# A Mamba-2 scan and a hard-swish MLP on one core: the first MLP product from three products of 12-bit parts instead of seven half-products

## The chip, the core and the metric

The kernel runs on one core of one Trainium2 chip. The core has five engines that run side by side and meet through semaphores: in this kernel PE multiplies matrices into PSUM (used as eight banks of 128 partitions by 512 float32 values), ACT and DVE work element by element on SBUF and PSUM, POOL works element by element on SBUF, and SP only issues DMAs. PEld is the row of PE's weight loads: a matmul has a loaded operand, here of up to 128x128, and an operand that is streamed past it, here of up to 512 columns. The metric is the device time of one execution in microseconds.

## What is computed

Two stages follow each other. The first is a Mamba-2 scan of 4 batches, 8 heads, 768 positions, head width 32 and state width 16. The second is an MLP over the 3072 resulting rows of 256 values:

```python
h = x @ w_in                     # 3072x256 times 256x2048
relu6 = np.clip(h + 3.0, 0.0, 6.0)
g = h * relu6 / 6.0
return (g @ w_out)               # 3072x2048 times 2048x256
```

The weights come in as float64 and are decoded on the chip to float32; x, a, B and C are float32. The change is about `x @ w_in`.

## The kernel before

The 768 positions are cut into 6 blocks of 128; with 4 batches a block holds 512 rows of the MLP. Block k has three kinds of work, and the program interleaves them by hand: the scan of the block after it (k+1) and preparations for the one after that (k+2) are put between the products of the MLP of block k. The order of the instructions on each engine is the order in which the program writes them; nothing is planned by a scheduler.

**Block 0** is simple. `mlp_in` (line 621) makes h in 16 slices of 128 columns (f = 0 to 15), each from two float32 matmuls (two, as 256 input values are two halves of 128, j = 0 and 1), while the weights are still being decoded by `decode` (line 189). `first_out` (line 711) then makes the output product, four batches times four weight chunks, one step (i, b) after the other; between the steps the loop in the last part of the program puts the scan of block 1, four calls for sums of w_out (`weight_sums`, line 737) and two calls for sums of w_in (`in_weight_sums`, line 640).

**Blocks 1 to 5** make the first product by a seven-product scheme (a Strassen form on 2x2 blocks). Two slices of h belong to one step s (0 to 7), one even and one odd. Each of the four parts (even or odd, first or second 256 of the 512 rows) is a sum over j; instead of eight half-products of 256 columns, `lead`, `early`, `middle` and `last` (lines 669 to 698) issue seven through `half_product`, some on sums of weights (tile w_sum and two temporary ones) and sums of rows (tile ts, by `sum_y`, line 656), and ACT and DVE carry intermediate sums between the banks. `lead` of the next step runs one step ahead, and `lead(c, 0)` of the next block is put near the end of the previous block's output product. A step holds two PSUM banks; three pairs of banks rotate (f0/f2, f1/f3, y0/y1).

The slice h then goes through `ramp` (line 700, ACT: relu of h/6 + 1/2 into the tile gT) and `times_ramp` (line 705, DVE: the minimum with 1, times h). POOL makes sums of these slices for the output product (`g_sums`, line 756), which is a seven-product scheme too: `wide_units` (line 835) for blocks 1 to 4 and `out_units` (line 768) for block 5. While `wide_units` yields its steps i = 0 to 13, the loop puts in the scan of the next block: `scores` and `multiply` at i = 2 or 3, `decay_ends` of the block after it (32 short exponentials on ACT and 4 products on POOL in all) at i = 2 to 5, `results` (`mix` on PE, `keep` with four copies by ACT into yT, and `sum_y`) at i = 6 or 7, and `turn_all` at i = 9.

The loads go through SP's queue in program order: `load_bc` (B once with tokens first, and 16 DMAs that bring C and B in squares), `load_x`, and `rows` (the decay rows L and eto). The stores of a block, 32 of them, go through the same queue. The pools `loads` and `att` have two buffers for each tag unless a tile says otherwise.

Of the kernel before, what the change touches and what calls it, by code (L numbers as in the profile page):

```python
# [11 lines left out]
BF16 = mybir.dt.bfloat16  # L12
AF = mybir.ActivationFunctionType
# [7 lines left out]
def kernel(  # L21
# [24 lines left out]
    nc = tc.nc  # L46
# [38 lines left out]
    def load_bc(c):  # L85
# [21 lines left out]
        Bs[c] = tokens_first(B, nc.scalar if c == 0 else nc.sync, name="B")  # L107
        if c == 0:
            bcs[c] = [pairs_first(C), Bs[c]]
        elif c < TURN:  # L110
            bcs[c].append(Bs[c])
        elif c > TURN:
            bcs[c] = [pairs_first(C), pairs_first(B)]
        else:
            return lambda: bcs.update({c: [pairs_first(C), pairs_first(B)]})

    def load_x(c):
        sl = slice(c * P, (c + 1) * P)
        xts[c] = loads.tile([P, NB * NH, D], FP32, name="xt")
        nc.sync.dma_start(out=xts[c], in_=x[:, :, sl, :].rearrange("b h s d -> s (b h) d"))  # L120

    w_in = const.tile([P, NK, DF], FP32, name="w_in")
    w_sum = const.tile([P, NF // 2, P], FP32, name="w_sum")
    w_out = const.tile([P, NF, DM], FP32, name="w_out")
    NP = 4
    FP = NF // NP
    NRAW = 3
# [61 lines left out]
    def decode(i):  # L189
# [42 lines left out]
        if i < NP:  # L232
            dst = w_in[:, :, i * FP * P:(i + 1) * FP * P]
# [159 lines left out]
    def ends(c, b):  # L393

        if b == 0:
            bss[c] = att.tile([P, G, N], FP32, name="bs")
# [214 lines left out]
    def keep(c):  # L611

        yTs[c] = att.tile([P, NK, NB, P], FP32, name="yT")
# [7 lines left out]
    def mlp_in(k, f):  # L621
        h = ps.tile([P, NK, 2 * P], FP32, name="h", tag=f"f{f % 4}")
        for j in range(NK):
            nc.tensor.matmul(  # L624
                out=h.rearrange("p r i -> p (r i)"), lhsT=w_in[:, j, f * P:(f + 1) * P],
# [11 lines left out]
    wi = w_in.rearrange("p k (j e c) -> p k e j c", e=2, c=P)  # L637
    in_sums, y_sums, evens, odds, parts_of = {}, {}, {}, {}, {}

    def in_weight_sums():  # L640
        for h in range(2):
            js = slice(h * NJ // 2, (h + 1) * NJ // 2)
            a11, a12, a21, a22 = (wi[:, k, e, js] for e in range(2) for k in range(2))
            s1, s2 = (att.tile([P, NJ // 2, P], FP32, name="w_sum", tag=t) for t in ("ws", "we"))
            s4 = w_sum[:, js]
            for o, p_, q_, op in ((s1, a21, a22, ALU.add), (s2, s1, a11, ALU.subtract),
                                  (s4, a12, s2, ALU.subtract), (a21, a11, a21, ALU.subtract)):
                nc.vector.tensor_tensor(out=o, in0=p_, in1=q_, op=op)
            for n, t in ((1, s1), (2, s2), (3, a21), (4, s4)):
# [487 lines left out]
```

## Time and profile before

| what | value |
|---|---|
| median of 3 runs | 354.44 us (354.25 to 355.27) |
| the profiled execution | 354.35 us, of which the span of its instructions is 352.6 us |
| PE busy | 344.0 us, 98% of the span |
| DVE, ACT, POOL busy | 228.7, 179.4, 138.8 us (65%, 51%, 39%) |
| first product of blocks 1 to 5 (PE chain, tiles even and odd) | 20.1% and 14.7% of the span |
| granted PE clock | 0.999 of full speed |

In a row of the groups, the numbers are the tile written and the tiles read, the shapes, the count, the busy time in us, the mean duration of one in ns, and after the bar the idle time of the engine just before. A matmul's duration includes its passage through the array, so it is longer than the distance between the starts of two matmuls in a row; the distance is what a stream of them costs, and it is read from the chain, where a stretch of PE work has a length and a count. For ACT and DVE the same is read from the starts in the timeline.

### The profile page before, as it was taken

The page shows a single profiled execution, that of the slowest core. Times are in us where ns is not written, and L with a number is a line of the kernel's source. Part 1 is how long each engine was busy: PE and PEld are TensorE (multiplying, and loading weights), DVE is VectorE, ACT ScalarE, POOL GpSimd, SP SyncE. Part 2 cuts the span into 40 slices and gives each one's busy share as a digit, 9 for nine tenths or more (in the row PEclk, how much of TensorE's full clock was granted, in tenths as well). Part 3 has the DMA queues.
Part 4 walks back from the last instruction along what each step waited for, and adds up shares of the span by engine and source line. Part 5 has one row for each costly group of instructions (what it writes and reads, how often), then busy time and mean ns, then how long its engine had stood idle before and what let it go on. Part 6 is the DMA issues. An engine that isn't in the chain of part 4 may idle for free.

```text
span 352.6 us, 8499 instructions
## 1 busy us (share of the span) xinstructions
PE 344.0 (98%) x3448; PEld 281.9 (80%) x3448; DVE 228.7 (65%) x426; ACT 179.4 (51%) x394; POOL 138.8 (39%) x139
## 2 busy tenths in 40 slices
PE   6899999999999999999999999999999999999996
PEld 2554458888888888888888888888888888888996
DVE  6699999975788628786438787436787322688111
ACT  3778887258775731664741565551575011466100
POOL 3300000362499612099513099610078600068700
PEclk9999999999999999999999999999999999999999
DMA  8988979602900293255034256001200001200000
GB/s 168 190 301 166 214 268 149 86 16 77 164 1 6 57 167 70 35 69 83 2 82 91 35 67 90 4 4 17 34 9 0 2 5 19 37 7 0 2 30 32
DMA packets 89607, 25.18 MB, mean 71 GB/s; under 512 B 82208, under 2 KB 85952, under 8 KB 89056
## 3 DMA queue, kind: packets, MB, share of 16 engines
q1 hardware_dynamic: 85184, 23.33, 35.3%
q10 hardware_dynamic: 4384, 1.31, 1.7%
q8 instruction: 27, 0.44, 0.6%
q14 instruction: 12, 0.10, 0.1%
HBM read 21.33 MB, written 3.29 MB: 70 GB/s over the span
## 4 chain that ended last, share of the span: by engine, by line
PE 94%; DMA 3%; DVE 1%; SPq 1%; issue 0%; DVEq 0%
PE even L666 20%; PE odd L666 15%; PE wb L844 12%; PE wc L844 8%; PE o L721 8%; PE h L624 8%; PE wa L844 8%; PE oa L780 4%; PE ob L780 4%; PE y L602 3%; PE y L505 2%; PE cb L532 2%; DMA raw<-in_moe_w_in_dram 2%; DMA pairs<-in_C_dram 1%; PE y L546 1%; SPq L100 1%
## 5 line engine op out<-in xcount | busy, mean ns | idle before, releaser
L766 POOL TENSOR_TENSOR s<-gT 128x512 f32<-128x512 f32 x20 | 25.4, 1271 | 82.4 <-DVE gT L707 82.4
L666 PE MATMUL even<-ts,w_sum 128*128 128x256 f32 x160 | 48.1, 382 | 0.0
L702 ACT ACTIVATE gT<-odd,half 128x512 f32<-128x512 f32 x40 | 27.5, 688 | 33.8 <-DVE odd L695 33.8
L666 PE MATMUL odd<-yT,w_in 128*128 128x256 f32 x160 | 41.1, 379 | 0.0
L681 ACT COPY even<-odd 128x512 f32<-128x512 f32 x40 | 23.0, 574 | 27.7 <-PE odd L666 25.0
L666 PEld LDWEIGHTS even<-ts,w_sum 128*128 128x128 f32 x160 | 30.0, 190 | 5.1 <-ACT up L688 1.3
L707 DVE SCALAR_TENSOR_TENSOR gT<-gT,odd 128x512 f32<-128x512 f32 x40 | 27.5, 688 | 9.9 <-ACT gT L702 9.9
L666 PEld LDWEIGHTS odd<-yT,w_in 128*128 128x128 f32 x160 | 30.4, 190 | 4.1
L387 ACT ACTIVATE L<-L,cum_n 128x64 f32<-128x64 f32 x128 | 31.5, 340 | 0.0
L844 PE MATMUL wb<-s,w_out 128*128 128x256 f32 x128 | 30.7, 382 | 0.0
L707 DVE SCALAR_TENSOR_TENSOR gT<-gT,even 128x512 f32<-128x512 f32 x40 | 27.2, 679 | 4.4 <-ACT gT L702 4.4
L702 ACT ACTIVATE gT<-even,half 128x512 f32<-128x512 f32 x40 | 27.8, 695 | 4.4 <-PE even L666 4.4
L721 PE MATMUL o<-w_out,gT 128*128 128x256 f32 x128 | 28.7, 381 | 0.0
L405 POOL TENSOR_TENSOR tmp<-state,eto 128x256 f32<-128x256 f32 x5 | 3.4, 684 | 62.1 <-ACT eto L391 62.1
L624 PE MATMUL h<-yT,w_in 128*128 128x512 f32 x64 | 27.7, 594 | 0.0
L721 PEld LDWEIGHTS o<-w_out,gT 128*128 128x128 f32 x128 | 24.1, 190 | 3.7 <-issue 0.5
L682 DVE COPY up<-odd 128x256 f32<-128x256 f32 x40 | 16.9, 424 | 15.4 <-ACT even L681 14.6
L844 PEld LDWEIGHTS wb<-s,w_out 128*128 128x128 f32 x128 | 24.0, 190 | 3.4
L766 POOL TENSOR_TENSOR s<-s,gT 128x512 f32<-128x512 f32 x20 | 25.9, 1295 | 1.6
L766 POOL TENSOR_TENSOR gT<-gT 128x512 f32<-128x512 f32 x20 | 25.5, 1274 | 0.0
L766 POOL TENSOR_TENSOR s<-gT,s 128x512 f32<-128x512 f32 x20 | 25.5, 1273 | 0.0
L160 POOL TENSOR_SCALAR_AFFINE_SELECT L<-L 64x1024 f32<-64x1024 f32 (+1 forms) x16 | 18.9, 1182 | 15.3 <-DMA L<-cum_d 14.9
(150 smaller groups left out, 666.1 us busy)
## 6 DMA issues: line engine op xcount, KB each, us to landing
raw<-in_moe_w_out_dram SPq DMA_DIRECT2D x4, 1024.0 KB
L<-cum_d SPq DMA_DIRECT2D x8, 512.0 KB
xt<-in_x_dram SPq DMA_DIRECT2D x6, 512.0 KB
raw<-in_moe_w_in_dram SPq DMA_DIRECT2D x3, 1024.0 KB
out_dram<-back SPq DMA_DIRECT2D x128, 16.0 KB
pairs<-in_C_dram SPq DMA_DIRECT2D x40, 32.0 KB
eto<-cum_e SPq DMA_DIRECT2D x20, 64.0 KB
B<-in_B_dram SPq DMA_DIRECT2D x5, 256.0 KB
```

The source lines that it names most:

```text
L160: nc.gpsimd.affine_select(out=t[rows], in_=t[rows], pattern=pattern, compare_op=ALU.is_ge, fill=-1e5, base=base, channel_multiplier=-1)
L387: nc.scalar.activation(Ls[c][:, b, h], Ls[c][:, b, h], AF.Exp, bias=cum_n[:, c, g:g + 1])
L624: nc.tensor.matmul(out=h.rearrange("p r i -> p (r i)"), lhsT=w_in[:, j, f * P:(f + 1) * P], rhs=yTs[k][:, j].rearrange("p b i -> p (b i)") ...
L666: nc.tensor.matmul(out=bank[:, r], lhsT=lhsT, rhs=rhs, start=start, stop=True, skip_group_check=True)
L681: nc.scalar.copy(out=even, in_=odd[:, 1:2].to_broadcast([P, 2, 2 * P]))
L682: nc.vector.tensor_copy(out=up[:, 1], in_=odd[:, 0])
L702: nc.scalar.activation(gTs[k][:, f], h.rearrange("p r i -> p (r i)"), AF.Relu, bias=half, scale=1.0 / 6.0)
L707: nc.vector.scalar_tensor_tensor(out=g, in0=g, scalar=1.0, in1=h.rearrange("p r i -> p (r i)"), op0=ALU.min, op1=ALU.mult)
L721: nc.tensor.matmul(out=o[:, b % 2], lhsT=gTs[0][:, f, b * P:(b + 1) * P], rhs=w_out[:, f], start=(f == 0 and b % 2 == 0), stop=True, skip_ ...
L766: nc.gpsimd.tensor_tensor(out=o, in0=p_, in1=q_, op=op)
L780: nc.tensor.matmul(out=bank[:, slot], lhsT=lhs[:, j], rhs=rhs[:, j], start=(clear and j == 0), stop=True, skip_group_check=True)
L844: nc.tensor.matmul(out=bank[:, slot], lhsT=lhs[:, j], rhs=rhs[:, j], start=(clear and j == 0), stop=True, skip_group_check=True)
```

## The change

In blocks 1 to 5 the seven-product scheme of the first product goes. Each operand x is split in two parts of 12 bits, hi = x(1 - e/2) rounded to the type float32r with e = 2^-12, and lo = x - hi; the lo of the weights is multiplied by 1/e. A third operand, called less, combines the two: lo - hi of the weights (with the scaled lo), and e hi - lo of the rows. For each slice f there are three products with 512 streamed columns and two halves j each: hi times hi and lo times lo into one bank (`squares`), then that bank is multiplied in place by 1 + e on ACT, or on DVE for every fourth slice and the first two of block 1 (`enlarge`), and then less times less is accumulated on it (`cross`). That sum is hi hi + hi lo + lo hi + lo lo. All these matmuls have float32r operands; in the kernel before no matmul has.

Slices run in the order squares(f), cross(f-2), enlarge(f), factor(f-2), with six banks in rotation; `factor` is `ramp` and `times_ramp`. `lead` now means the first two slices' squares. The split of the weights (`in_parts`, four chunks in two parts each) is put between the steps of block 0's output product, and the split of the rows (`split_y`) takes the place of `sum_y`. The tiles B, xt, bs and yT have one buffer instead of two, w_in becomes four tiles that the parts of later chunks overwrite, ob, res, x1 and u of the outputs share tags with tiles of `wide_units`, and t2 and t4 of the w_out sums get buffers of their own. Loads move: x of the next block is loaded at slice 2 of a block, where before x of the block after it was; B and C of block 2 are loaded after step (1, 3) of block 0. The four w_out sums move from block 0 (and one from block 1's output product) to slices 4, 7, 9 and 12 of block 1. In block 0, conceal, turn, wake, decay and ends are put at other steps, and in later blocks `decay_ends` is one step later (i = 3 to 6).

```diff
-        Bs[c] = tokens_first(B, nc.scalar if c == 0 else nc.sync, name="B")
+        Bs[c] = tokens_first(B, nc.scalar if c == 0 else nc.sync, name="B", bufs=1)
         if c == 0:
             bcs[c] = [pairs_first(C), Bs[c]]
         elif c < TURN:
             bcs[c].append(Bs[c])
-        elif c > TURN:
+        else:
             bcs[c] = [pairs_first(C), pairs_first(B)]
-        else:
-            return lambda: bcs.update({c: [pairs_first(C), pairs_first(B)]})
 
     def load_x(c):
         sl = slice(c * P, (c + 1) * P)
-        xts[c] = loads.tile([P, NB * NH, D], FP32, name="xt")
+        xts[c] = loads.tile([P, NB * NH, D], FP32, name="xt", bufs=1)
...
-    w_in = const.tile([P, NK, DF], FP32, name="w_in")
-    w_sum = const.tile([P, NF // 2, P], FP32, name="w_sum")
-    w_out = const.tile([P, NF, DM], FP32, name="w_out")
     NP = 4
     FP = NF // NP
+    w_in = [const.tile([P, NK, FP * P], FP32, name="w_in", tag=f"w{i}") for i in range(NP)]
...
-            bss[c] = att.tile([P, G, N], FP32, name="bs")
+            bss[c] = att.tile([P, G, N], FP32, name="bs", bufs=1)
...
-        yTs[c] = att.tile([P, NK, NB, P], FP32, name="yT")
+        yTs[c] = att.tile([P, NK, NB, P], FP32, name="yT", bufs=1)
...
-    def sum_y(k):
-        ts = att.tile([P, 3, 2 * P], FP32, name="ts", bufs=1)
-        t1, t2, t4 = (ts[:, i] for i in range(3))
-        t3 = y_half(k, 0, 1)
-        y_sums[k] = {1: t1, 2: t2, 3: t3, 4: t4}
-        for o, p_, q_ in ((t1, t3, y_half(k, 0, 0)), (t3, y_half(k, 1, 1), t3),
-                          (t2, y_half(k, 1, 1), t1), (t4, y_half(k, 1, 0), t2)):
-            nc.vector.tensor_tensor(out=o, in0=p_, in1=q_, op=ALU.subtract)
...
-    def half_product(bank, r, lhsT, rhs, start=False):
-        nc.tensor.matmul(
-            out=bank[:, r], lhsT=lhsT, rhs=rhs, start=start, stop=True, skip_group_check=True)
-
-    def lead(k, s):
...
-        half_product(odd, 1, wi[:, 0, 0, s], y_half(k, 0, 0), start=True)
-        half_product(odd, 0, in_sums[3][s], y_sums[k][3])
-        nc.scalar.copy(out=even, in_=odd[:, 1:2].to_broadcast([P, 2, 2 * P]))
-        nc.vector.tensor_copy(out=up[:, 1], in_=odd[:, 0])
-
-    def early(k, s):
-        even = evens[k, s]
-        half_product(even, 0, wi[:, 1, 0, s], y_half(k, 1, 0))
-        half_product(even, 1, in_sums[2][s], y_sums[k][2])
-        nc.scalar.copy(out=parts_of[k, s][:, 0], in_=even[:, 1])
-
-    def middle(k, s):
-        even, odd, up = evens[k, s], odds[k, s], parts_of[k, s]
-        half_product(odd, 0, wi[:, 1, 1, s], y_sums[k][4])
-        half_product(even, 1, in_sums[1][s], y_sums[k][1])
-        nc.vector.tensor_tensor(out=odd[:, 0], in0=odd[:, 0], in1=up[:, 0], op=ALU.add)
-        nc.vector.tensor_tensor(out=odd[:, 1], in0=even[:, 1], in1=up[:, 1], op=ALU.add)
-
-    def last(k, s):
-        half_product(evens[k, s], 1, in_sums[4][s], y_half(k, 1, 1))
+    EPS = 2.0 ** -12
+    w_parts, y_parts, hs_ = {}, {}, {}
+
+    def in_parts(i):
+        n = FP * P
+
+        def one(pool, tag):
+            t = pool.tile([P, NK, n], F32R, name="w_part", tag=tag)
+            return [t[:, j] for j in range(NK)]
+
+        def two(tag):
+            return [att.tile([P, n], F32R, name="w_part", tag=tag) for _ in range(NK)]
+
+        hi = one(const, f"w{i - 1}" if i else "hi")
+        lo = one(const, f"lo{i}") if i < 2 else one(att, "wm") if i == 2 else two("ws")
+        less = one(const, f"less{i}") if i < 2 else one(att, "wm") if i == 2 else two("we")
+        for j in range(NK):
+            nc.scalar.activation(hi[j], w_in[i][:, j], AF.Copy, scale=1.0 - EPS / 2)
+            (nc.vector if j and i > 1 else nc.gpsimd).tensor_tensor(
+                out=lo[j], in0=w_in[i][:, j], in1=hi[j].bitcast(FP32), op=ALU.subtract)
+        yield
+        for j in range(NK):
+            nc.scalar.activation(lo[j], lo[j].bitcast(FP32), AF.Copy, scale=1.0 / EPS)
+            nc.vector.tensor_tensor(
+                out=less[j], in0=lo[j].bitcast(FP32), in1=hi[j].bitcast(FP32), op=ALU.subtract)
+        w_parts[i] = (hi, lo, less)
+        yield
+
+    def split_y(k):
+        hi = const.tile([P, NK, TB], F32R, name="y_hi", tag=f"w{NP - 1}")
+        lo = att.tile([P, NK, TB], F32R, name="y_lo", bufs=1)
+        less = att.tile([P, NK, TB], F32R, name="y_less", bufs=1)
+        for j in range(NK):
+            y = yTs[k][:, j].rearrange("p b i -> p (b i)")
+            nc.scalar.activation(hi[:, j], y, AF.Copy, scale=1.0 - EPS / 2)
+            nc.vector.tensor_tensor(
+                out=lo[:, j], in0=y, in1=hi[:, j].bitcast(FP32), op=ALU.subtract)
+            nc.vector.scalar_tensor_tensor(
+                out=less[:, j], in0=hi[:, j].bitcast(FP32), scalar=EPS,
+                in1=lo[:, j].bitcast(FP32), op0=ALU.mult, op1=ALU.subtract)
+        y_parts[k] = (hi, lo, less)
+
+    def part_products(k, f, n, m, start=False):
+        w, y = w_parts[f // FP][n], y_parts[k][m]
+        for j in range(NK):
+            nc.tensor.matmul(
+                out=hs_[k, f], lhsT=w[j][:, f % FP * P:(f % FP + 1) * P], rhs=y[:, j],
+                start=(start and j == 0), stop=True, skip_group_check=True)
+
+    def squares(k, f):
+
+        pool, tag = ((ps, "f0"), (ps, "f1"), (ps, "f2"), (ps, "f3"), (ps_y, "y0"), (ps_y, "y1"))[f % 6]
+        hs_[k, f] = pool.tile([P, TB], FP32, name="h", tag=tag)
+        part_products(k, f, 0, 0, start=True)
+        part_products(k, f, 1, 1)
+
+    def enlarge(k, f):
+
+        h = hs_[k, f]
+        if f % 4 == 3 or k == 1 and f < 2:
+            nc.vector.tensor_scalar(
+                out=h, in0=h, scalar1=1.0 + EPS, scalar2=None, op0=ALU.mult)
+        else:
+            nc.scalar.activation(h, h, AF.Copy, scale=1.0 + EPS)
+
+    def cross(k, f):
+        part_products(k, f, 2, 2)
+
+    def factor(k, f):
+        ramp(k, f, hs_[k, f])
+        times_ramp(k, f, hs_[k, f])
+
+    def lead(k):
+        for f in range(2):
+            squares(k, f)
+            enlarge(k, f)
...
-                lead(c, 0)
+                lead(c)
...
-            ob = ffn.tile([P, 2, DM], FP32, name="ob", bufs=2)
+            ob = ffn.tile([P, 4, DM], FP32, name="ob", tag=("wide", "back")[b // 2])[:, :2]
...
-        sum_y(c)
+        split_y(c)
...
-            sums, sums_in = weight_sums(), in_weight_sums()
+            sums, ins = weight_sums(), [in_parts(i) for i in range(NP)]
+            next(ins[0])
...
-                    elif (i, b) == (1, 0):
-                        next(sums_in)
-                        next(sums_in)
-                    elif (i, b) == (2, 0):
+                    elif (i, b) in ((0, 1), (0, 3), (1, 1), (1, 2), (2, 1), (2, 2), (3, 0)):
+                        next(ins[{1: 1, 3: 0, 5: 1, 6: 2, 9: 2, 10: 3, 12: 3}[NB * i + b]])
+                    elif (i, b) == (1, 3):
                         turn(c, 1)
                         wake(c)
                         turn(c, 0)
-                        load_pairs()
-                        for p in range(2):
-                            conceal(ahead, p)
+                        load_bc(ahead)
+                        conceal(ahead, 1)
+                    elif (i, b) == (1, 0):
+                        conceal(ahead, 0)
                     elif (i, b) == (2, 3):
+                        decay(ahead, 0)
                         scores(c)
                         multiply(c)
+                        decay(ahead, 1)
                         renew(c)
-                        decay_ends(ahead, 0)
-                        decay_ends(ahead, 1)
-                        next(sums)
-                    elif (i, b) == (3, 0):
-                        next(sums)
-                        decay_ends(ahead, 2)
                     elif (i, b) == (3, 1):
                         results(c)
-                        next(sums)
-                        decay_ends(ahead, 3)
+                        decay(ahead, 2)
+                    elif (i, b) == (3, 2):
+                        decay(ahead, 3)
+                        from_start(ahead)
                     elif (i, b) == (3, 3):
-                        from_start(ahead)
+                        for q in range(NB):
+                            ends(ahead, q)
             rows(ahead + 1)
             continue
-        for s in range(NJ):
-            early(k, s)
-            if s == 0:
-                if ahead < NC:
-                    load(ahead)
+        for f in range(2, NF):
+            squares(k, f)
+            if f == 2:
                 if c < NC:
+                    load_x(c)
                     carry(c)
-            if s < NJ - 1:
-                lead(k, s + 1)
-            if s:
-                last(k, s - 1)
-                ramp(k, 2 * s - 2, evens[k, s - 1])
-            middle(k, s)
-            if s:
-                times_ramp(k, 2 * s - 2, evens[k, s - 1])
-            ramp(k, 2 * s + 1, odds[k, s])
-            times_ramp(k, 2 * s + 1, odds[k, s])
-            if s in (1, 3) and ahead < NC:
-                conceal(ahead, s // 2)
-            if s in (2, 4, 6):
-                g_sums(k, s - 2)
+                if k > 0 and ahead < NC:
+                    load_bc(ahead)
+            cross(k, f - 2)
+            enlarge(k, f)
+            factor(k, f - 2)
+            if f in (3, 7) and ahead < NC:
+                conceal(ahead, f // 4)
+            if f in (6, 10, 14):
+                g_sums(k, f // 2 - 3)
+            if k == 1 and f in (4, 7, 9, 12):
+                next(sums)
+        cross(k, NF - 2)
         for i, _ in enumerate((wide_units if c < NC else out_units)(k)):
             if i == 0:
-                s = NJ - 1
-                last(k, s)
-                ramp(k, 2 * s, evens[k, s])
-                times_ramp(k, 2 * s, evens[k, s])
-                g_sums(k, s - 1)
+                cross(k, NF - 1)
+                factor(k, NF - 2)
+                factor(k, NF - 1)
+                g_sums(k, NJ - 2)
...
-                if ahead < NC and 2 <= i < 6:
-                    decay_ends(ahead, i - 2)
+                if ahead < NC and 3 <= i < 7:
+                    decay_ends(ahead, i - 3)
...
-                    lead(c, 0)
+                    lead(c)
```

## The prediction

> **What bounds the kernel now.** I read the page's busy table and slices, then the chain that ended last, then the single rows of the two products, then the timelines of ACT, DVE, POOL and SP around a block's first product.
>
> ```profile
> PE 344.0 (98%) x3448; PEld 281.9 (80%) x3448; DVE 228.7 (65%) x426; ACT 179.4 (51%) x394; POOL 138.8 (39%) x139
> ...
> PEclk9999999999999999999999999999999999999999
> ...
> PE 94%; DMA 3%; DVE 1%; SPq 1%; issue 0%; DVEq 0%
> ```
>
> PE is busy in 98% of the span at full clock, and the chain is PE for 94%: time comes off only where PE's instructions get fewer or shorter, and every wait put on PE comes on top. The next two views are the chain by line, and single rows by tile and line.
>
> ```profile
> by line: PE even L666 20.1%; PE odd L666 14.7%; PE wb L844 12.2%; PE wc L844 8.1%; PE o L721 7.9%; PE h L624 7.8%; PE wa L844 7.8%; PE oa L780 3.6%; PE ob L780 3.5%; PE y L602 2.7%; PE y L505 2.0%; PE cb L532 1.9%; DMA raw<-in_moe_w_in_dram
> ...
> 22.65 27.66 PE h L624 x64
> ...
> 329.79 1.79 PE ob L780 x16
> ```
>
> ```profile
> L624 PE MATMUL h<-yT,w_in x64: 592/592/697, 22.6 to 49.7; 128*128 128x512 f32 x64
> L666 PE MATMUL odd<-yT,w_in x160: 379/379/379, 82.6 to 319.8; 128*128 128x256 f32 x160
> L350 PE MATMUL d<-less,split x8: 379/494/634, 7.4 to 13.1; 128*128 128x512 bf16 x8
> L780 PE MATMUL oa<-w_out,gT 128*128 128x128 f32 x64 | 7.8, 276 | 0.0
> L780 PEld LDWEIGHTS oa<-w_out,gT 128*128 128x128 f32 x64 | 7.6, 192 | 0.2
> ```
>
> The first product of blocks 1 to 5 (tiles even and odd) holds 20.1 + 14.7 = 34.8% of 352.6, 122.7 us, 24.5 a block. It has 560 records: 5 blocks, 8 steps, 7 half-products, each float32 product as two records. The h rows give the price of streaming: 27.66 / 64 = 0.432 us for a 512-column float32 record, and half of it, 0.216, for a 256-column one (560 x 0.216 = 121.0, so waits are only 1.7 of the 122.7). A bf16 record of 512 columns lasts at its shortest 379 ns, just as a float32 record of 256 columns: one record of float32 streams its columns twice, bf16 once. The last two rows show that loads hide: records of 128 columns follow each other every 1.79 / 16 = 0.112 us though each load is put at 192 ns.
>
> **The matmuls.** Removed: 560 records of 0.216. Added: 5 blocks x 16 slices x 3 products x 2 halves = 480 of 512 columns with float32r operands, a type that no row shows. One end is the bf16 row, one passage, 0.216 (a 379 ns row lies at that distance); the other is float32 with 512 columns, 0.432. I take 0.216: a float32 product shows four passages (two records of two), which is two halves of each operand against two of the other; an operand of 12 bits has one half, and bf16 is the only row with one record and one passage for a product. Then 480 x 0.216 = 103.7 us against 122.7: 19.0 us less, 3.8 a block. By the other end it is 84.7 us more. The Trainium skill (FP8 and Floating Point Precision, TensorE Precision Notes) says that true float32 takes four passes and that there is a reduced form which reads four bytes and cuts them to 22 bits; the four passes agree with two records of two passages here, and no run here shows the reduced form's rate.
>
> The same skill (TensorE: Matmul & The Clock Gate, Back-to-back issue gap) gives 131 ns as the sustained spacing at 512 columns, by which the stage would cost 480 x 0.131 = 62.9 us and the whole some 295; but the rows here never stream 512 columns in less than 0.216, so I go by the rows; it gets 0.01 of the rest named below.
>
> **ACT and DVE beside them.** Per slice ACT does ramp and, for three of four, enlarge. Rows: ramp from PSUM 0.69, the PSUM to PSUM copy 0.57. In the timeline ramp's successor starts 0.59 later:
>
> ```profile
> 145.77 0.69 ACT L702 ACTIVATE gT<-odd,half 128x512 f32<-128x512 f32 x1 [0.76 <-DVE odd L695]
> 146.36 0.36 ACT L688 COPY up<-even 128x256 f32<-128x256 f32 x1
> ```
>
> So ACT needs 1.75 x 0.59 = 1.03 to 1.75 x 0.69 = 1.21 us for a slice of 6 x 0.216 = 1.30 on PE; DVE 1.25 x 0.60 to 0.69 = 0.75 to 0.86. The bounds of enlarge, 0.5 (the copy's distance) and 0.69, both keep ACT under PE, so I cost it at nothing; its cover is 0.1 to 0.27 us a slice. Between squares(f) and cross(f) lie cross(f-2), squares(f+1) and cross(f-1), 0.43 + 0.86 + 0.43 = 1.7 us, against 0.6 for enlarge. A bank is taken again after six slices, 7.8 us; its use takes 3.9 us to the end of cross, then 0.6 to 1.3 each for ramp and times_ramp, some 6. Both hidden. In exchange ACT loses two copies a step (0.57 + 0.37) and DVE three short operations.
>
> **split_y.** Two ACT and four DVE operations of 0.59 to 0.72 replace four DVE ones of 0.43. In blocks 2 to 5 yT is ready at 128.5 in the trace's second block and lead starts at 136.6; 0.6 + 4 x 0.6 = 3.0 us fit with 5 to spare, also with decay_ends a step later (2.0 us of ACT, eight exponentials). If that cover is gone, each us late is a us in each block. At the first seam it is not there: yT is complete at 82.0 and lead starts at 82.8. hi is then ready at 82.6 and 83.2, lo of the second half behind less of the first at 84.5; PE would want it at 83.7. I take 1.2 us once; ends 0 and 4 (ACT late as below).
>
> **Block 0.** in_parts adds 16 ACT operations of 0.59 to 0.72, 9.4 to 11.5 us, to 21.2 busy of the 33.4 us of the output product:
>
> ```profile
> 50.30:83.70 33.40, 33.40 (x458) 29.05 (x457) 28.65 (x45) 21.15 (x51) 9.53 (x12) 1.00 0.58 99
> ```
>
> That is full, but what must be in time is the scan only. ACT ends the decode at 61.2, one chunk's hi ahead of it makes it 62.4 (w_out's last chunk then at 66, wanted at 71). Four more pairs of its operations (1.2 each) and a wait for POOL's lo bring it to 68, where turn's copies began at 66.3; B, C and the start values are ready at 70, bs on POOL (6 more products of 1.27 and conceal before it) at 73.3, where 71.3 was. scores starts at 72 and its state products at 73.5: just in time, cost nothing, ends 0 and 3 us. DVE loses eight w_in sums and three w_out sums there (10 us) and gets about 8. The four w_out sums (1.22 each) lie in block 1, where DVE has 20.7 less 12 us free; they are wanted 4 us into the output product.
>
> **POOL.** g_sums takes 5.0 us for four slices, PE 5.2. With conceal in between POOL ends some 10.5 us after the output product's start, where it ended 9.5 after; the sums that it makes last are wanted from 16 us on. Nothing.
>
> **Loads on SP.** load_x(c) now comes behind the stores, ahead of B and the squares. In the trace B went out at 149.6 and the product needing x came at 169: 15 us of cover after shortening, while the longest that SP was held by one such load is 7.5 (an estimate of its length; the landing is not in the trace). One buffer for xt, B, bs and yT adds waits on readers that ended in the block before. B(2) in block 0 waits for ends(1), to 73; behind it stand 16 squares (11 us of issue), the stores of ob and rows(3), so L for conceal(3) lands perhaps 3 us after the 94 of before, and POOL's g_sums in block 1 starts later; by the count above it has more than that to spare. turn_all(2) reads the squares at 105.
>
> **Sum.** 354.35 - 19.0 + 1.2 = 336.6 us in the profiled execution's terms (span some 334.8; 1.75 us lie around it), 0.09 below the median of 354.44, which I leave out. 0.3% is 1.1 us here, about what a measurement of this kernel can tell from no change.
>
> **The rivals.**
> 1. Weight loads come into the open (slower). A float32r matmul streams once per load, a float32 product twice for two. If a load can't run beside the matmul before it, each costs 0.216 + 0.112 (the shortest distance of loads) = 0.328, and 480 make 157.5: 354.35 + 34.8 + 1.2 = 390. It decides against the change from 0.253 us a matmul, 37 ns of open load. Against it: the float32 rows hide a load behind every 0.216 and even every 0.112. The Trainium skill (TensorE: Matmul & The Clock Gate, The mechanism) has loads overlap running matmuls only with another row group; by that rule these full-height loads would lie open, which the L780 rows contradict for float32. Chance 0.08.
> 2. float32r takes two passages or more: 480 x 0.432 = 207.4, 440 us. For it: it reads four bytes a value as float32 does. Chance 0.05.
> 3. The change is as fast on PE, but block 0 is late: ACT is 92 to 98% taken there and scores, results and lead hang on it. Upper ends above: 4 + 3 instead of 1.2, 342. Chance 0.14.
> 4. ACT becomes the pace of the stage. It needs over 0.74 us for each of 28 operations in 20.7 us; at 0.80 the stage is 22.4 and the time 336.6 + 5 x 1.65 = 345. Against it 0.59. Chance 0.08.
>
> **Numbers.** The forecast, 336.6 (own range 334 to 339.5), has 0.62; the rest, 0.03, is waits that I don't see. Rivals 3 and 4 take the range to 349, and without 1 and 2 some 0.17 lie outside 333 to 349. Faster 0.84, same 0.02, slower 0.14.
>
> **What would show it.** In the profile after: rows on part_products, 480, of 379 ns with starts 0.216 apart and idle near zero; the five stretches of the first product near 20.7 us; the output products unchanged at about 27 to 30; ACT waiting for PE in the stage, not PE for ACT; a gap of a us on PE at lead of block 1. Rows much over 379 ns, or PEld loads that alternate with them, would make the prediction wrong; a PE idle on ACT enlarge or DVE less would say rival 4 or 3.

## The result, and the profile after

The changed kernel takes 350.5 us (349.98 to 351.36), the kernel before 354.69 beside it: a ratio of 0.988, 95% interval 0.986 to 0.991. That is faster by 1.2%, clear of the noise and in the direction of the forecast, but far from its 5%: 336.6 us was predicted, and 350.5 lies above the range of 334 to 339.5. The profiled execution took 351.36 us with a span of 349.6; it is the longest of the four.

The page of the changed kernel, busy times, granted clock by slice, and shares of the chain that ended last:

```profile
PE 335.5 (96%) x3368; PEld 268.9 (77%) x3368; DVE 216.5 (62%) x330; ACT 191.6 (55%) x398; POOL 154.7 (44%) x145
...
PEclk9969999998999999999999999999999999999999
...
PE 79%; DVE 9%; ACT 5%; DMA 3%; issue 2%; POOL 1%; SPq 1%; DVEq 0%; POOLq 0%
```

PE no longer holds 94% of the chain but 79%, and two slices show a lowered clock: something other than PE now sets a part of the time, early in the span. The chain by line, and a stretch of it (start, length, count):

```profile
by line: PE h L687 31.9%; PE wb L861 12.3%; PE wc L861 8.2%; PE wa L861 7.9%; PE oa L797 3.6%; PE ob L797 3.6%; PE y L600 2.9%; PE y L503 2.3%; DVE gT L726 2.2%; PE cb L530 2.1%; PE o L739 2.1%; ACT we L221 1.9%; DMA raw<-in_moe_w_in_dram 1
...
146.07 19.96 PE h L687 x86
```

The first product of blocks 1 to 5 (L687) now takes 31.9% of 349.6 = 111.5 us, where it took 122.7: 11.2 less, not 19.0. One matmul costs 19.96 / 86 = 0.232 us, not 0.216. The output products are as they were (12.3 + 8.2 + 7.9 = 28.4% of 349.6, 99.3 us; 99.1 before). The single rows:

```profile
L721 ACT ACTIVATE gT<-h,half 128x512 f32<-128x512 f32 x96 | 65.2, 684 | 21.9 <-PE h L687 20.0
...
L705 ACT ACTIVATE h<-h 128x512 f32<-128x512 f32 x58 | 33.8, 582 | 43.1 <-PE h L687 43.1
L687 PE MATMUL h<-y_hi,w_part 128*128 128x512 f32 x160 | 52.3, 408 | 0.0
L687 PE MATMUL h<-y_lo,w_part 128*128 128x512 f32 x160 | 50.2, 394 | 0.0
L687 PE MATMUL h<-y_less,w_part 128*128 128x512 f32 x160 | 50.0, 398 | 0.0
```

ACT waits for PE (43.1 and 20.0 us); PE never idles ahead of these matmuls. So the stage goes at PE's own pace, and that pace is slower than was forecast: means of 394 to 408 ns in place of bf16's 379.

The rest went in block 0. The start of `lead` for block 1 in the chain, first before, then after:

```profile
82.80 0.86 PE odd L666 x4
```

```profile
90.87 1.98 PE h L687 x8
```

From block 0's first product to there, before took 82.80 - 22.65 = 60.15 us, after 90.87 - 24.3 = 66.6. PE in the trace after, and then DVE and POOL ahead of it (start, length, operation, and in brackets the idle time and what ended it; csT is the scan's turned C, which `scores` needs):

```profile
78.08 1.00 PE L503 MATMUL y<-csT,state 32*64 32x64 f32 x25 [4.49 <-DVE csT L447]
```

```profile
60.87 1.76 DVE L201 TENSOR_SCALAR wm<-raw 128x1024 uint32<-128x1024 uint32 x1
62.55 1.76 DVE L228 TENSOR_TENSOR we<-we,ws 128x1024 uint16<-128x1024 uint16 x1
64.34 1.22 DVE L236 SCALAR_TENSOR_TENSOR w_out<-wm,we 128x1024 f32<-128x1024 f32 x1
65.49 2.30 DVE L205 SCALAR_TENSOR_TENSOR wm<-raw,wm 128x1024 f32<-128x1024 uint32 x1
67.71 1.75 DVE L228 TENSOR_TENSOR we<-we,ws 128x1024 uint16<-128x1024 uint16 x1
69.50 2.05 DVE L236 SCALAR_TENSOR_TENSOR w_out<-wm,we 128x1024 f32<-128x1024 f32 x1
71.47 5.14 DVE L665 TENSOR_TENSOR w_part<-w_part 128x512 fp32r<-128x512 f32 x4
76.53 0.90 DVE L660 TENSOR_TENSOR w_part<-w_in,w_part 128x512 fp32r<-128x512 f32 x1
77.35 0.68 DVE L447 TENSOR_TENSOR csT<-t_ps,eto 128x512 f32<-128x512 f32 x1
```

```profile
60.80 2.96 POOL L660 TENSOR_TENSOR w_part<-w_in,w_part 128x512 fp32r<-128x512 f32 x2 [44.06 <-ACT w_part L659]
64.50 4.41 POOL L660 TENSOR_TENSOR w_part<-w_in,w_part 128x512 fp32r<-128x512 f32 x2 [0.74 <-ACT w_part L659]
68.87 3.69 POOL L158 TENSOR_SCALAR_AFFINE_SELECT L<-L 64x1024 f32<-64x1024 f32 x2
```

While POOL works beside it, first on the split weights' lo and then on the masks of L (L158), five of DVE's decode operations go from 0.69 to 1.76 us or from 1.22 to 2.05 and 2.30, by 5.1 us together. The decode ends at 71.5 instead of 64.6 us (1.7 of it a later start); four subtractions of less then take 5.14 us instead of some 2.5, one lo stands ahead of csT, and PE waits 4.49 us for csT. The trace of before already had rows of this kind, which the prediction passed over: the same DVE operation takes 0.69 us while POOL rests and 0.99 beside POOL's first product of the scan.

```profile
63.49 1.22 DVE L238 SCALAR_TENSOR_TENSOR w_out<-wm,we 128x1024 f32<-128x1024 f32 x1
65.36 0.69 DVE L648 TENSOR_TENSOR w_sum<-w_sum,w_in 128x512 f32<-128x512 f32 x1
68.01 0.99 DVE L648 TENSOR_TENSOR w_sum<-w_sum,w_in 128x512 f32<-128x512 f32 x1
```

```profile
67.52 0.94 POOL L405 TENSOR_TENSOR tmp<-state,eto 128x256 f32<-128x256 f32 x1 [50.67 <-ACT eto L391]
```

Granted clock in stretches of the trace after (columns: the stretch and its length, busy us and count of PE, PEld, DVE, ACT, POOL; then the clock, the DMA share and GB/s):

```profile
16.00:20.00 4.00, 3.59 (x100) 2.01 (x85) 3.69 (x7) 2.02 (x4) 0.74 (x1) 0.57 0.98 336
20.00:24.00 4.00, 4.00 (x157) 3.23 (x157) 3.93 (x7) 0.98 (x3) 0.00 (x0) 0.58 1.00 403
74.00:78.00 4.00, 0.00 (x0) 0.00 (x0) 4.00 (x6) 1.17 (x3) 4.00 (x6) 1.00 0.00 0
78.00:80.00 2.00, 1.92 (x75) 1.92 (x80) 2.00 (x3) 2.00 (x8) 1.93 (x3) 0.50 0.47 45
80.00:82.00 2.00, 2.00 (x101) 1.58 (x87) 2.00 (x3) 1.07 (x6) 2.00 (x2) 0.66 1.12 106
```

Behind the wait the clock stands at 0.50 and 0.66 for 4 us, which stretches the next PE work by some 1.5 us; with some 0.4 on mix that makes the 6.4 us of block 0. The lowered clock at 16 to 24 us costs 1.7 us at the start (first product at 24.3 instead of 22.65). It belongs to this execution and not to the change: of the kernels below, which begin in the same way, the one with the order alone has it (first product at 24.25) and the one with bf16 parts has not (22.59).

So from 354.35: -11.2 (first product), +6.4 (block 0), +1.7 (the start) = 351.25, against 351.36.

### The profile page after: what moved, and what is told of

It reads as the page before. It is cut to its first block, busy times and chain, and to the rows that moved or that the text cites. A ratio compares the mean times of both kernels' runs of the same rounds, so it can differ in the third digit from the quotient of the medians.

```text
span 349.6 us, 8199 instructions
## 1 busy us (share of the span) xinstructions
PE 335.5 (96%) x3368; PEld 268.9 (77%) x3368; DVE 216.5 (62%) x330; ACT 191.6 (55%) x398; POOL 154.7 (44%) x145
## 4 chain that ended last, share of the span: by engine, by line
PE 79%; DVE 9%; ACT 5%; DMA 3%; issue 2%; POOL 1%; SPq 1%; DVEq 0%; POOLq 0%
PE h L687 32%; PE wb L861 12%; PE wc L861 8%; PE wa L861 8%; PE oa L797 4%; PE ob L797 4%; PE y L600 3%; PE y L503 2%; DVE gT L726 2%; PE cb L530 2%; PE o L739 2%; ACT we L221 2%; DMA raw<-in_moe_w_in_dram 2%; POOL w_part L660 1%; DVE wm L205 1%
## 5 line engine op out<-in xcount | busy, mean ns | idle before, releaser
L726 DVE SCALAR_TENSOR_TENSOR gT<-gT,h 128x512 f32<-128x512 f32 x96 | 65.3, 686 | 42.1 <-ACT gT L721 40.5
L721 ACT ACTIVATE gT<-h,half 128x512 f32<-128x512 f32 x96 | 65.2, 684 | 21.9 <-PE h L687 20.0
L705 ACT ACTIVATE h<-h 128x512 f32<-128x512 f32 x58 | 33.8, 582 | 43.1 <-PE h L687 43.1
L687 PE MATMUL h<-y_hi,w_part 128*128 128x512 f32 x160 | 52.3, 408 | 0.0
L687 PE MATMUL h<-y_lo,w_part 128*128 128x512 f32 x160 | 50.2, 394 | 0.0
L687 PE MATMUL h<-y_less,w_part 128*128 128x512 f32 x160 | 50.0, 398 | 0.0
L687 PEld LDWEIGHTS h<-y_lo,w_part 128*128 128x128 f32 x160 | 30.0, 187 | 7.7 <-DVE y_lo L677 0.3
L687 PEld LDWEIGHTS h<-y_less,w_part 128*128 128x128 f32 x160 | 29.9, 188 | 7.0 <-DVE h L702 0.3
L687 PEld LDWEIGHTS h<-y_hi,w_part 128*128 128x128 f32 x160 | 30.1, 188 | 6.5
L158 POOL TENSOR_SCALAR_AFFINE_SELECT L<-L 64x1024 f32<-64x1024 f32 (+1 forms) x16 | 22.0, 1375 | 11.6 <-DMA L<-cum_d 5.8
L622 PEld LDWEIGHTS h<-yT,w_in 128*128 128x128 f32 x64 | 12.1, 190 | 14.9 <-issue 12.9
```

Source lines behind the costliest of these rows:

```text
L158: nc.gpsimd.affine_select(out=t[rows], in_=t[rows], pattern=pattern, compare_op=ALU.is_ge, fill=-1e5, base=base, channel_multiplier=-1)
L622: nc.tensor.matmul(out=h, lhsT=w_in[f // FP][:, j, f % FP * P:(f % FP + 1) * P], rhs=yTs[k][:, j].rearrange("p b i -> p (b i)"), start=(j ...
L687: nc.tensor.matmul(out=hs_[k, f], lhsT=w[j][:, f % FP * P:(f % FP + 1) * P], rhs=y[:, j], start=(start and j == 0), stop=True, skip_group_ ...
L705: nc.scalar.activation(h, h, AF.Copy, scale=1.0 + EPS)
L721: nc.scalar.activation(gTs[k][:, f], h, AF.Relu, bias=half, scale=1.0 / 6.0)
L726: nc.vector.scalar_tensor_tensor(out=g, in0=g, scalar=1.0, in1=h, op0=ALU.min, op1=ALU.mult)
```

## Why is a matmul 0.232 us? bf16 parts, and half the columns

Theory: float32r itself is streamed more slowly than bf16, and the forecast's counting of passages is right. Rivals: something in this stage (the six banks, the order of the products) would slow any type; or a fixed cost for each matmul; or the weight loads, 187 to 188 ns each, set the pace. The first run stores the same parts as bf16, which keeps fewer bits of them; the product is then less precise. (The rest of its edit takes away the reinterpretations of the parts as float32.)

```diff
-F32R = mybir.dt.float32r
+F32R = mybir.dt.bfloat16
...
```

> The three parts are held in bfloat16 instead of float32r, so the products carry fewer bits; everything else stays. Theory A (the 0.233 us between two part products belongs to the float32r type: its 187 ns load is not fully hidden or its columns stream slower): the spacing falls to 0.216 us, the stage from 22.4 to 20.7 us a block. Rival B (any 512-column matmul in one passage with a load of its own takes 0.233 here, float32 hides it only since it has two passages a load): the spacing stays at 0.233.

Measured: 339.85 us in one run. A stretch of its chain, and its rows:

```profile
89.94 9.28 PE h L687 x43
```

```profile
L687 PEld LDWEIGHTS <-w_part 128*128 128x128 bf16 x480 | 46.9, 98 | 55.2 <-issue 0.2
L687 PE MATMUL h<-y_lo,w_part 128*128 128x512 bf16 x156 | 46.8, 379 | 0.5
```

9.28 / 43 = 0.2158 us a matmul in the same order, banks and waits, and rows of 379 ns: the forecast's price, to the digit, for another type. (480 x 0.2158 = 103.6; with block 0's stretch of 64.7 us here, 354.35 - 19.1 + 4.6 = 339.85.) What is slow is float32r. The loads take half as long too, 98 ns, so this run alone doesn't part the stream from the loads. The second run cuts each matmul in two of 256 columns, with a load each.

```diff
-            nc.tensor.matmul(
-                out=hs_[k, f], lhsT=w[j][:, f % FP * P:(f % FP + 1) * P], rhs=y[:, j],
-                start=(start and j == 0), stop=True, skip_group_check=True)
+            for r in range(2):
+                rs = slice(r * 2 * P, (r + 1) * 2 * P)
+                nc.tensor.matmul(
+                    out=hs_[k, f][:, rs], lhsT=w[j][:, f % FP * P:(f % FP + 1) * P],
+                    rhs=y[:, j, rs],
+                    start=(start and j == 0 and r == 0), stop=True, skip_group_check=True)
```

> Each part product is cut in two of 256 columns, each with its own load: 960 matmuls instead of 480, the same columns streamed. Theory A1 (a fixed 17 to 20 ns a matmul that the next load leaves open): 0.107 + 0.020 = 0.125 us apart, the stage 16 x 12 x 0.125 = 24.0 us a block, the whole some 8 us over the changed kernel's 350.5. Rival A2 (float32r streams its columns 8% slower): 0.117 apart, the stage as now, 22.4. Rival A3 (the load sets the pace, one every 0.233): 0.233 apart, the stage 44.7 us, the whole 112 us longer.

Measured: 357.51 us in one run; from the chain and the rows:

```profile
93.89 20.46 PE h L689 x172
...
236.25 1.80 issue
```

```profile
L689 PE MATMUL h<-y_hi,w_part 128*128 128x256 f32 x320 | 52.8, 287 | 0.0
L689 PEld LDWEIGHTS h<-y_hi,w_part 128*128 128x128 f32 x320 | 44.3, 189 | 0.5
```

20.46 / 172 = 0.119 us for 256 columns. With as many loads as matmuls, loads that set the pace would have left 0.232; a fixed excess of 16 ns would give 0.108 + 0.016 = 0.124, an excess that goes with the columns 0.116. It lies between, nearer to the columns. The float32 records of the kernel before settle more: each streams its columns twice beside one load of 190 to 192 ns, and they follow each other every 0.112 us for 128 columns and every 0.216 for 256. As many columns streamed beside a load of the same length thus take float32r 0.119 and 0.232, 6 and 7% more. So the excess goes with what is streamed, and a load of that length doesn't make it by itself. Why float32r streams more slowly isn't shown; a part of its loads in it isn't ruled out, since no run here mixes the types. (The whole is 6.2 us over the changed kernel's profiled execution: 2.7 in the stage, a stall of 1.80 us in block 3, and some 1.7 by a lowered clock behind it.)

## Why is block 0 late? The lo on DVE, the order, and POOL in the kernel before

Theory: POOL and DVE hold each other up. Rival: the order of the pieces, which puts ACT's, POOL's and DVE's work of the split ahead of the scan's. The first run makes every lo on DVE, 0.69 us each, so DVE gets six more operations; the second keeps POOL and moves the pieces of `in_parts` back, to where they don't stand beside the decode.

```diff
-            (nc.vector if j and i > 1 else nc.gpsimd).tensor_tensor(
+            nc.vector.tensor_tensor(
```

> The weights' lo is subtracted on DVE for all chunks; before, six of eight were on POOL. Theory (POOL and DVE lengthen each other when they run side by side in block 0, so that csT comes 4.5 us late for scores): DVE's decode rows return from 1.76 and 2.30 to 0.69 and 1.22 us there, though DVE gets six more operations of 0.69; the wait before scores shrinks from 4.5 us to under 1.5, and the whole is 3 to 5 us shorter than the changed kernel, 345.5 to 347.5. Rival (DVE simply has too much to do before csT): the added 4 us of DVE make the wait longer, 352 or more.

```diff
-                    elif (i, b) in ((0, 1), (0, 3), (1, 1), (1, 2), (2, 1), (2, 2), (3, 0)):
-                        next(ins[{1: 1, 3: 0, 5: 1, 6: 2, 9: 2, 10: 3, 12: 3}[NB * i + b]])
+                    elif (i, b) in ((0, 1), (2, 0), (2, 1), (2, 2), (3, 0)):
+                        for q in {1: (1, 0), 8: (1,), 9: (2,), 10: (2, 3), 12: (3,)}[NB * i + b]:
+                            next(ins[q])
```

> Only the order in block 0 changes: the second part of chunk 1 and both parts of chunks 2 and 3 come after turn, so that turn's csT has less ahead of it on DVE; POOL keeps its subtractions. If the place in DVE's queue is what makes csT late, the wait of 4.5 us goes nearly whole (346 to 347). If the lengthening by POOL is, the decode still ends at 71 us instead of 64 and bs is late on POOL, so that some 2 us of the wait stay: 348 to 349.

Measured, with every lo on DVE: 345.96 us (345.53 to 346.16), ratio 0.972 (0.966 to 0.979) to before; a second time, later, 345.62 (345.14 to 346.63), ratio 0.973 (0.968 to 0.977). From the first run, DVE's operations between 28 and 72 us, and PE's wait:

```profile
L201 DVE TENSOR_SCALAR wm<-raw 128x1024 uint32<-128x1024 uint32 x6 | 4.1, 686 | 0.0
L228 DVE TENSOR_TENSOR we<-we,ws 128x1024 uint16<-128x1024 uint16 x6 | 4.1, 686 | 0.0
L660 DVE TENSOR_TENSOR w_part<-w_in,w_part 128x512 fp32r<-128x512 f32 x6 | 3.9, 684 | 0.0
```

```profile
73.61 0.61 PE L503 MATMUL y<-csT,state 32*64 32x64 f32 x25 [1.66 <-DVE csT L447]
```

These lines of the decode are back at their old durations (in the changed kernel the first two had means of 867 and 1041 ns there); two operations elsewhere in it are still longer, 1.37 us in place of 0.42 and 2.04 in place of 1.22, beside POOL's masks of L. The wait falls from 4.49 to 1.66 us, no lowered clock follows it, and `lead` starts at 84.97: block 0's stretch is 62.3 us, 2.1 over before in place of 6.4. DVE has more work and is done sooner.

With the order alone: 351.64 us (351.15 to 353.43), ratio 0.989 (0.983 to 0.995), no better than the changed kernel. The wait before scores did fall, and came back behind it:

```profile
74.67 0.61 PE L503 MATMUL y<-csT,state 32*64 32x64 f32 x25 [1.18 <-DVE csT L447]
...
85.73 2.31 PE L600 MATMUL y<-L,xt 64*32 64x64 f32 x128 [4.95 <-DVE mid L554]
```

Here ACT scales chunk 2's lo as soon as POOL has made it, and waits 9.81 us for that, with the scan's copies queued behind; DVE's lo of chunk 3 waits for ACT, and the start values (mid) wait behind DVE's. Both expected times (346 to 347, 348 to 349) missed: a piece moved off one wait stands in the next.

Then both: every lo on DVE, and chunk 2's second piece and chunk 3's first behind multiply.

```diff
-            (nc.vector if j and i > 1 else nc.gpsimd).tensor_tensor(
+            nc.vector.tensor_tensor(
...
+                    elif (i, b) in ((0, 1), (2, 0), (2, 1), (3, 0)):
+                        for q in {1: (1, 0), 8: (1,), 9: (2,), 12: (3,)}[NB * i + b]:
...
+                        next(ins[2])
+                        next(ins[3])
```

> The changed kernel with the weights' lo on DVE and another order in block 0: the second part of chunk 1 and the first of chunk 2 come after turn, the second of chunk 2 and the first of chunk 3 after scores and multiply. Theory (what is left of block 0's delay is the in-order queues of DVE and ACT ahead of csT and of the products with cb): neither scores nor mix waits over 0.5 us, lead of block 1 starts at 83 to 83.5 us, the whole 344 to 345. Rival (the split's operations don't fit ahead of lead at all): what the start gains, PE loses waiting for the rows' split or for less of chunk 3: 346 or more.

Measured: 349.57 us (348.14 to 351.47), ratio 0.985 (0.982 to 0.988): worse than the lo on DVE alone. Scores and mix start without a wait, but `lead` waits for the split of the rows:

```profile
86.72 1.02 PE L687 MATMUL h<-y_hi,w_part 128*128 128x512 f32 x2 [1.91 <-ACT y_hi L676]
...
88.78 0.79 PE L687 MATMUL h<-y_lo,w_part 128*128 128x512 f32 x1 [0.80 <-DVE y_lo L677]
```

```profile
88.00:90.00 2.00, 1.23 (x3) 1.04 (x4) 1.80 (x4) 2.00 (x10) 0.51 (x1) 0.59 0.00 0
90.00:92.00 2.00, 2.00 (x6) 1.58 (x6) 0.99 (x2) 1.50 (x6) 0.84 (x2) 0.55 0.03 8
```

ACT makes chunk 3's scaling ahead of the copies into yT, and y_hi is late; the clock is then at 0.59 and 0.55 for 4 us. A last run of this kind puts the split out in three pieces (hi; lo; scale and less), chunk 3's lo behind multiply and its scaling at step (3, 0):

```diff
-            (nc.vector if j and i > 1 else nc.gpsimd).tensor_tensor(
+        yield
+        for j in range(NK):
+            nc.vector.tensor_tensor(
                 out=lo[j], in0=w_in[i][:, j], in1=hi[j].bitcast(FP32), op=ALU.subtract)
...
+            next(ins[0])
...
+                    elif (i, b) in ((0, 1), (0, 3), (1, 1), (2, 0), (2, 1), (2, 2), (3, 0)):
+                        for q in {1: (1, 1), 3: (0,), 5: (1,), 8: (2, 2), 9: (2,), 10: (3,),
+                                  12: (3,)}[NB * i + b]:
...
+                        next(ins[3])
```

> Every lo of the weights on DVE, and the split of the weights put out in three pieces (hi; lo; scale and less): chunk 2 whole after turn, chunk 3's hi at step (2, 2), its lo behind multiply, its scale and less at step (3, 0). In the run with every lo on DVE alone (345.96 us) PE still waited 1.66 us before scores, and in the run that moved the pieces too (349.57) no wait stood at scores or mix, but 2.7 us at lead. Theory (what is left is DVE's and ACT's turn at the scan, to be had by order): csT is ready a us or more sooner, the wait before scores falls to 0.5 us or less, none comes up at mix or lead, lead starts at 83.5 to 84.3, and the whole takes 344.3 to 345.3 us. Rival (the pieces don't fit ahead of lead; the stall only moves): a wait of 1 us or more on y_hi, y_lo or mid stands at mix or at lead, and the whole takes 346 us or more.

> The kernel with every lo on DVE once more, beside the run with three pieces, so that the two are compared on the same chip: 345.5 to 346.2 us by its first runs. Both theories give the same here; if the rival on the three pieces holds, this one is the faster of the two.

Measured: 346.23 us (345.44 to 349.95), beside 345.62 for the plain lo on DVE: nothing won.

```profile
74.35 0.61 PE L503 MATMUL y<-csT,state 32*64 32x64 f32 x25 [0.63 <-DVE csT L447]
...
87.28 0.50 PE L689 MATMUL h<-y_lo,w_part 128*128 128x512 f32 x1 [0.80 <-DVE y_lo L679]
```

The 1.66 us before scores became 0.63, and 0.80 stands at `lead`: less than the rival's 1 us, but the time isn't better than the plain one's, as the rival has it. None of the three orders won time; each moved the wait.

Does POOL hold DVE up by itself, without float32r and the new order? The kernel before, with six subtractions of 128x512 on POOL beside the decode whose results nobody reads:

```diff
-        t3 = const.tile([P, NJ, P], FP32, name="t3")
+        t3 = spare
...
+    spare = const.tile([P, NJ, P], FP32, name="t3")
+
+    def beside(n):
+        for _ in range(n):
+            nc.gpsimd.tensor_tensor(
+                out=spare[:, :FP].rearrange("p (k j) c -> p k (j c)", k=2),
+                in0=w_out[:, 0:2], in1=w_out[:, 2:4], op=ALU.subtract)
...
+            beside(6)
```

> The kernel before, with six idle POOL subtractions of 128x512 float32 from SBUF to SBUF whose results nobody reads, put beside the decode from about 50 us on. Theory (POOL and DVE products from SBUF hold each other up): DVE's decode rows that run beside them take 1.76 to 2.3 us in place of 0.69 to 1.22, POOL's 1.7 to 2.3 instead of 1.27, and the decode ends at 68 to 70 us instead of 64.6; the whole 0 to 3 us longer. Rival (the rows were long in the changed kernel for float32r or for what they waited on): all stay at 0.69, 1.22 and 1.27 us.

Measured: 360.26 us (359.64 to 361.0), ratio 1.015 (1.013 to 1.018). DVE, POOL and PE:

```profile
52.63 1.75 DVE L203 TENSOR_SCALAR wm<-raw 128x1024 uint32<-128x1024 uint32 x1
...
58.42 2.18 DVE L238 SCALAR_TENSOR_TENSOR w_out<-wm,we 128x1024 f32<-128x1024 f32 x1
...
61.31 0.69 DVE L203 TENSOR_SCALAR wm<-raw 128x1024 uint32<-128x1024 uint32 x1
```

```profile
49.75 9.77 POOL L756 TENSOR_TENSOR t<-w_out 128x512 f32<-128x512 f32 x6 [33.12 <-DVE w_out L238]
```

```profile
60.66 10.59 PE L721 MATMUL o<-w_out,gT 128*128 128x256 f32 x40 [3.15 <-DVE w_out L238]
```

Until POOL ends at 59.5 us the decode has long durations like the changed kernel's (1.75 and 2.18), and right behind it the old ones (0.69). POOL's own take 1.63 each, against 1.27 for its g_sums in before. The decode ends at 69.4 instead of 64.6, PE waits 3.15 us for w_out, and 40 matmuls take 10.59 us instead of 8.64, at a clock of 0.50 and 0.68: 5.1 of the 5.5 us. The decode's end is as expected (68 to 70); the whole is longer than the 0 to 3 us that were expected, since the expectation left out the clock behind the wait. That POOL holds DVE up is shown from both sides: by taking work from POOL, and by giving it some.

The Trainium skill (SBUF — State Buffer, SBUF: two separate sides) says that GpSimd shares one pair of ports with DVE operations that run in a two-port mode or have two SBUF inputs (these only against a GpSimd operation that reads SBUF), and that whoever comes first holds it for the whole instruction. The rows of the changed kernel agree with waiting for an instruction: +1.06 on operations of 0.69, +0.83 to +1.08 on those of 1.22, that is a like amount for short and long, not a like ratio. Also, DVE's gT operations, one of whose two inputs lies in PSUM, keep their 0.69 beside POOL (mean 686 ns over the 96).

Both causes taken away at once, on the kernel with every lo on DVE and the pieces moved, parts in bf16 as above:

> The same with the three parts in bfloat16, so the products carry fewer bits; a probe of the sum. Theory (the forecast of 336.6 failed by two things alone, the float32r spacing and block 0's delay): both gone, the spacing is 0.216 and the whole 336 to 337.5. If a third cost hides in the later blocks: 339 or more.

Measured: 338.37 us (337.77 to 339.45), ratio 0.954 (0.951 to 0.958), about 1 us above the 336 to 337.5 that were expected and under the 339 that would have meant a third cost. What is left is at `lead`:

```profile
85.72 0.38 PE L687 MATMUL h<-y_lo,w_part 128*128 128x512 bf16 x1 [0.94 <-DVE y_lo L677]
```

It is within 1.8 us of the forecast of 336.6, so no third cost above that is hidden behind the two.

## Why the prediction was wrong

Right was: the direction; one passage for a float32r product (rival 2, 440 us, is out); loads beside the stream (rival 1, 390 us, decided from 0.253 us a matmul; measured 0.232, of which at most 0.016 could be open load); ACT and DVE beside PE in the stage (ACT's enlarge 0.58 us, ramp 0.69, waiting for PE, rival 4 out); split_y in blocks 2 to 5, POOL's g_sums and the loads on SP, which cost PE nothing. The full-height loads run beside matmuls, as the prediction held against the row-group rule of the Trainium skill (TensorE: Matmul & The Clock Gate, The mechanism), and no stream of 512-column matmuls came near that page's 131 ns: 216 ns for bf16, 232 for float32r. (That section of the Trainium skill also lets a load into a background buffer go ahead, which the prediction left out; these rows contradict only its sentence without that condition.)

Wrong were two steps, and one was half right.

- **The matmuls.** "I take 0.216": the term of 480 x 0.216 = 103.7 us measured 111.5, +7.8. The mechanism was right, the size was off by 7%. The row it was read from is bf16's, and for bf16 it held; float32r has no row in the trace of before, and the ends, 0.216 and 0.432, were one and two passages with nothing between. The runs showed one passage at a pace 7% slower. A price only 16 ns higher takes 40% of the expected gain away, because the gain itself is a difference of two large terms, 122.7 and 103.7.
- **Block 0.** "just in time, cost nothing, ends 0 and 3": it cost 6.4 us. The step that failed is "w_out's last chunk then at 66", and with it "DVE loses eight w_in sums and three w_out sums there (10 us) and gets about 8". Each operation was priced by its row from a stretch where POOL stood still; the change puts POOL's lo beside the decode, and then DVE's take up to 1.1 us longer and POOL's 1.81 on the mean instead of 1.27. The last decode ended at 71.5. Rival 3 named the place, and that scores and lead hang on it, but blamed ACT, and at 342 us priced it at 7 us in place of 1.2. That this is near to the 6.4 is luck, since the cause was another. A chance of 0.14 was low for a step of which the prediction itself says that it has no slack.
- **The first seam.** 1.2 us were counted for split_y; the changed kernel shows 0.1. There ACT had got ahead while PE waited for csT, and its copies into yT wait for PE (0.32 and 0.74 us). Where PE's wait for csT is 0.63 us or gone, the stall is there: 0.80 and 0.94 us on y_lo. The mechanism was right.

In sum, 336.6 + 7.8 + 6.4 - 1.2 (in block 0's stretch already) + 1.7 (the clock at the start) = 351.3, against 351.36. With float32r at its measured price and every lo on DVE, a change of one line, the time is 345.6 to 346.0, the fastest of these kernels that keeps the float32r parts and 2.7% faster than before.

## What to carry to other kernels

A type or form that no row of the trace shows has no price yet: spread the range between its neighbours, and work out how much of the gain a few per cent on that price would eat. Before giving idle POOL some of DVE's work, look for a row where the two already run side by side, and count what each POOL operation adds to the DVE operations beside it; here 0.69 us more on DVE was cheaper than 1.8 us on an idle POOL. In a stretch without slack, moving pieces only moved the wait; what helped was to shorten the work.

## What was unexpected in the hardware

- float32r: 0.232 us for 512 streamed columns and 0.119 for 256, bf16 0.216 for 512; loads of 128x128 at 187 to 192 ns, against 98 in bf16.
- POOL beside DVE: 0.7 to 1.1 us more on most DVE operations between SBUF tiles that ran beside POOL's 128x512 subtractions or its masks, whether they last 0.42, 0.69 or 1.22, though not on all: one of 1.22 at 55.50 us in the kernel before with six subtractions kept its length. POOL's subtraction took 1.63 and 1.81 on the mean instead of 1.27.
- The granted clock behind a wait of PE: it stood at half for 3.41 us after 1.80, 2.85, 3.15 and 4.49 us of idle PE and after 1.91 and 0.80 close together, and for 6.83 us after 4.95; after 1.18 and 1.66 it stayed at full speed. The length of the wait alone doesn't decide: ahead of 15.4 us five traces have 2.23 to 2.55 us of idle PE and fall to half speed at 16.5 to 16.9, while four others have 2.29 to 2.54 there and don't. In each trace that shows changes of the clock they lie whole multiples of 3.41 us apart. Where the trace is cut into such stretches, PE was idle for 1.80 us or more in the one that ends where the clock falls, and for at most 1.68 in those behind which it stayed at full speed. So it fell where PE had been idle for about half of such a stretch or more; this is read from these traces, and no run was made to try it. The Trainium skill (TensorE: Matmul & The Clock Gate, Part 1: The HAM clock gate) lets half speed come after an idle window of some 3.4 us; the length of the stretch agrees, but here 1.80 us of idle in it were enough. A fall stretches the PE work behind the wait as well: the wait of 3.15 us cost 5.1.
